# First feed-forward product in pairs of 64-row products on doubled features, with the attention numerators and the output projection moved to the second product

## Chip, cores and metric

The kernel runs on one core of a Trainium2 chip. The metric is device microseconds of one execution, as the median of several timed runs. Engines are TensorE (PE, with its weight loads as PEld), VectorE (DVE), ScalarE (ACT), GpSimd (POOL) and SyncE (SP), which issues nearly all DMAs.

## What is computed

The reference is one transformer block over 2048 tokens of 576 features, 32 heads of 18, feed-forward width 4608. A conditioning vector c gives six vectors that scale, shift and gate. Cut to what matters:

```python
sa, ca, ga, sb, cb, gb = split(silu(c) @ w_mod, 6)
h = layernorm(x) * (1 + ca) + sa
x = x + ga * attention(h)          # per head, feature map softmax(q w), softmax(-q w);
                                   # num = phi_q (phi_k^T v), den = phi_q sum(phi_k); (num / den) @ wo
h = layernorm(x) * (1 + cb) + sb
x = x + gb * (maximum(h @ w1, 0) @ w2)
```

## The kernel before

**Stages.** A first stage (to about 91 us) follows a hand-written list of jobs, ORDER: projections for K, V and Q of all 16 token tiles of 128, the key sums, and the numerators, output projection, second normalisation and h of tiles 0 and 1. The softmaxed Q of later tiles are written to DRAM (q_out, L334) and read back (q_in, L337). Then a loop over eight blocks b of two tiles (256 tokens) does the feed-forward part. Block b runs l1 (the first product, L691) and l2 (the second, L724); the attention rest of the next two tiles is hooked into them.

**The first product.** Hidden features are cut into 36 chunks of 128, taken as 18 pairs j and j+18 (hf = 0, 1). The 576 features of h are four chunks of 128 and one of 64. l1_full (L667) multiplies the four full chunks (L673, 128 rows, 256 columns). l1_rest (L676) multiplies the last 64: h's 64 features lie twice, in partitions 0 to 63 and 64 to 127, and the weights w1b hold one half of the hidden features in each, so that two products of 64 rows (L680), one for each hf, run beside each other in the two halves of the array. Three groups g of six j each use bank pairs 0 to 2 of PSUM; in each group first a part of the full products, then all six L680 pairs, then the rest of the full products with relu (L683) after each u: ScalarE writes A11 (L687) and A2 (L688), VectorE U3 (L689), and after a group U2 (L711).

**The second product** uses a Strassen scheme: seven products of 18 matmuls (L735) with sums of the halves of A and of w2: T1 to T4 are differences of weights (t_part, L461), made by VectorE in block 0, A11 and A12 are changed in place by VectorE (L743, L747, L755). Bank X accumulates four products; ScalarE takes a snapshot of it after three of them (copy, L739). fin (L713) adds, gates and writes the results with VectorE (L718, L720) and GpSimd (L721, L722).

**Attention work in the loop.** q_next (L786) makes a tile's softmax sums and ratios (VectorE L282, L341; GpSimd L344, L289) and a DMA transpose into ET. attend (L795) is ten small matmuls (num_mm, L389), a division (num_o, L396 and L397), a copy of the last 64 features by ScalarE (L800), and a DMA transpose into oT. wo_rest and wo_full (L803, L810) project: a pair of 64-row products (L807) and eight full ones (L813). add_res (L411), bn (L238, L239) and norm2 (L816) normalise; a DMA transpose of five chunks puts the result into h2, and VectorE scales and shifts it (L851) in l2. Before, hooks place attend twice in l1 of the block ahead, the projections in its groups 1 and 2, and the scaling and q_next in l2.

**What sets the order.** The program's order is the order on each engine: every engine works its instructions in the order in which the code emits them, waiting on semaphores for data and for buffers. In ORDER the jobs ht (turn2, L526: transposes by TensorE), ha and hd (h2_e, L532: scale and shift by ScalarE and VectorE) make h of tiles 0 and 1 in bank pairs 2 (tile 1) and 0 (tile 0), just ahead of the Q projection of tile 15 (bank pair 1; Q of tile 14 is in pair 3) and the loop.

## Time and profile before

| | us |
|---|---|
| three timed runs | 387.99, 387.81, 387.46 (median 387.81) |
| profiled execution: its span | 386.3 |
| first product of block 0 starts | 91.28 |
| second product, blocks 0, 1 and 2, in the chain | 112.72, 149.44, 186.15 |
| one l2 (126 matmuls) | 15.4 |
| one l1 with the attention work in it | 21.3 |

The time of a run is that of the whole execution; the span runs from the first instruction of the program to the last, and 1.5 us of the median lie around it. In the rows of the profile, "x" counts instructions, then come busy us and the mean ns of one, then idle time before them and what released them. In the chain that ended last, a row is a start, a length and the work. PEld rows are weight loads, which run beside matmuls. A matmul's row is longer than the step to the next one, because matmuls overlap in the array: 0.273 against 0.109 us for L673. So steps, not rows, add up to TensorE's time.

### The profile page before, as it was taken

The numbers are of one execution on the slowest core, as the hardware profiler recorded it, in microseconds if no ns is written. First come the engines' busy times: TensorE is split into PE (matmuls) and PEld (weight loads), VectorE is DVE, ScalarE is ACT, GpSimd is POOL, SyncE is SP. The second block draws the span as 40 slices with busy tenths as digits, with TensorE's granted clock in tenths as the row PEclk, the third lists the DMA queues.
The fourth block names the chain that finished last, engine by engine and source line by source line (L and its number), as shares of the span: only waits on it lengthen the run. The fifth ranks groups of instructions, "written<-read, shape, count | busy, mean of one in ns | idle before, by whom it ended". The sixth has DMA issues, their size and how long they took to land.

```text
span 386.3 us, 8923 instructions
## 1 busy us (share of the span) xinstructions
PE 379.6 (98%) x3705; PEld 309.7 (80%) x3705; DVE 242.6 (63%) x470; ACT 156.7 (41%) x380; POOL 125.3 (32%) x195
## 2 busy tenths in 40 slices
PE   7999999999999999999999999999999999999995
PEld 4887778888887887788888888887888788778874
DVE  2898998784898666744764584567456735542333
ACT  2689997688540233034303420451054023302510
POOL 2088889830106400620160035004500540041023
PEclk9999999999999999999999999999999999999999
DMA  7995799798510524241233024212631221200001
GB/s 301 420 417 209 261 394 360 137 259 277 84 34 19 75 53 51 47 110 34 50 76 82 20 49 110 48 19 52 122 36 20 46 63 36 36 0 32 3 0 34
DMA packets 48940, 43.18 MB, mean 112 GB/s; under 512 B 39297, under 2 KB 41986, under 8 KB 48130
## 3 DMA queue, kind: packets, MB, share of 16 engines
q1 hardware_dynamic: 48610, 42.41, 39.4%
q8 instruction: 29, 0.48, 0.5%
q10 hardware_dynamic: 288, 0.19, 0.2%
q14 instruction: 13, 0.11, 0.1%
HBM read 27.38 MB, written 5.90 MB: 86 GB/s over the span
## 4 chain that ended last, share of the span: by engine, by line
PE 87%; DMA 4%; ACT 4%; DVE 3%; issue 1%; POOL 1%; SPq 0%; POOLq 0%; DVEq 0%
PE PS L673 33%; PE PS L735 31%; PE PS L272 9%; PE PS L680 5%; PE PS L813 4%; ACT RT L277 3%; DMA x_sb<-in_xk_dram 2%; PE PS L389 2%; DMA R<-in_wkT_dram 2%; PE PS L322 1%; DVE Rk L282 1%; PE PS L406 1%; DVE st L238 1%; ACT RT L511 0%; PE PS L807 0%
## 5 line engine op out<-in xcount | busy, mean ns | idle before, releaser
L673 PE MATMUL PS<-h,R 128*128 128x256 bf16 x1152 | 132.1, 273 | 0.0
L673 PEld LDWEIGHTS <-R 128*128 128x128 bf16 x1152 | 111.4, 98 | 14.1 <-issue 0.6
L735 PEld LDWEIGHTS <-RH 128*128 128x128 f16 x846 | 82.7, 98 | 20.7
L721 POOL TENSOR_TENSOR yt<-yt,gb_row 128x288 f32<-128x288 f32 x23 | 28.0, 1219 | 202.7 <-DVE yt L720 202.7
L687 ACT ACTIVATE RH<-PS 128x256 f16<-128x256 f32 x72 | 27.5, 382 | 110.6 <-PE PS L680 92.3
L735 PE MATMUL PS<-R,RH 128*128 128x288 bf16 (+1 forms) x558 | 72.1, 286 | 0.0
L689 DVE SCALAR_TENSOR_TENSOR RH<-PS,RH 128x256 f16<-128x256 f32 x72 | 28.6, 412 | 61.0 <-ACT RH L687 61.0
L688 ACT ACTIVATE RH<-PS 128x512 f16<-128x512 f32 x72 | 42.9, 596 | 5.5 <-PE PS L673 4.6
L277 ACT ACTIVATE RT<-PS,rs 128x576 bf16<-128x576 f32 x64 | 42.8, 742 | 2.3 <-PE PS L272 1.8
L735 PE MATMUL PS<-RT,RH 128*128 128x288 f16 x288 | 37.9, 286 | 0.0
L739 ACT ACTIVATE RS<-PS 128x288 f32<-128x288 f32 x24 | 9.8, 410 | 65.2 <-PE PS L735 65.2
L272 PE MATMUL PS<-RH,R 116*128 116x288 bf16 x240 | 32.5, 286 | 0.1
L272 PE MATMUL PS<-RH,RT 116*128 116x288 bf16 x240 | 31.9, 286 | 0.3
L720 DVE TENSOR_TENSOR yt<-PS,RS 128x288 f32<-128x288 f32 x23 | 10.5, 455 | 31.0 <-PE PS L735 21.9
L238 DVE BATCH_NORM_STATS2 st<-x_sb 128x6 f32<-128x288 bf16 x64 | 25.9, 447 | 4.0 <-DMA x_sb<-in_xk_dram 3.4
L272 PEld LDWEIGHTS <-RT 116*128 116x128 bf16 x240 | 22.9, 98 | 6.0 <-issue 0.5
L272 PEld LDWEIGHTS <-R 116*128 116x128 bf16 x240 | 22.7, 98 | 6.0 <-issue 0.5
L722 POOL TENSOR_TENSOR x_sb<-yt,x_sb 128x288 bf16<-128x288 f32 x31 | 22.7, 731 | 2.9 <-DVE yt L718 1.1
L282 DVE TENSOR_REDUCE Rk<-RT 128x64 f32<-128x1152 bf16 x16 | 21.3, 1336 | 0.9 <-ACT RT L277 0.7
L282 DVE TENSOR_REDUCE Rq<-RT 128x64 f32<-128x1152 bf16 x16 | 21.5, 1343 | 0.0
L680 PE MATMUL PS<-h,R 64*128 64x256 bf16 x288 | 19.9, 271 | 0.0
L411 DVE TENSOR_TENSOR x_sb<-x_sb,PS 128x576 bf16<-128x576 bf16 x16 | 12.1, 754 | 11.3 <-PE PS L813 10.2
(119 smaller groups left out, 418.8 us busy)
## 6 DMA issues: line engine op xcount, KB each, us to landing
R<-in_w1a_dram SPq DMA_DIRECT2D x4, 1152.0 KB, 8.2
eqd<-RT SPq DMA_DIRECT2D x12, 288.0 KB, 2.1
RT<-eqd SPq DMA_DIRECT2D x12, 288.0 KB, 3.5
R<-in_w2b_dram SPq DMA_DIRECT2D x2, 1296.0 KB, 8.1
R<-in_w2a_dram SPq DMA_DIRECT2D x3, 864.0 KB
out_dram<-x_sb SPq DMA_DIRECT2D x15, 144.0 KB, 2.1
RT<-in_xT_dram SPq DMA_DIRECT2D x2, 640.0 KB, 14.0
x_sb<-in_xk_dram SPq DMA_DIRECT2D x3, 288.0 KB
```

Source lines behind the costliest of these rows:

```text
L238: dve.bn_stats(out=s[:, hf, :], in_=x_sb[:, t, hf * HD:(hf + 1) * HD])
L272: pe.matmul(pr[:, k, 0:HD], lhsT=xt(t, ck), rhs=w[0:R, ck, k * HD:(k + 1) * HD], start=(ck == 0), stop=(ck == NC - 1))
L277: act.activation(out=E.rearrange("p (b h s e) -> p b h s e", b=2, s=2, e=DH)[:, :, :, s, :], in_=pr[:, :, 0:HD].rearrange("p b (h e) -> p ...
L282: dve.tensor_reduce(out=Rr, in_=E.rearrange("p (c e) -> p c e", e=DH), axis=AXX, op=ALU.add)
L673: pe.matmul(PS[:, 2 * u + hf, n * 256:n * 256 + 256], lhsT=w1a[:, ci, jj * P:(jj + 1) * P], rhs=hb[:, ci, :], start=(n == 0 and ci == 0), ...
L680: pe.matmul(PS[:, 2 * u + hf, n * 256:n * 256 + 256], lhsT=w1b[b0:b0 + 64, j * P:(j + 1) * P], rhs=hb[b0:b0 + 64, 4, :], start=False, stop ...
L687: act.activation(out=A11[:, j, :], in_=lo[:, :, 0, :], func=ACT.Relu)
L688: act.activation(out=A2[:, j, :, :], in_=PS[:, 2 * u + 1, :].rearrange("p (n s f) -> p n s f", n=2, s=2), func=ACT.Relu)
L689: dve.scalar_tensor_tensor(out=U3[:, j, :], in0=lo[:, :, 1, :], scalar=0.0, in1=A11[:, j, :], op0=ALU.max, op1=ALU.subtract)
L721: pool.tensor_tensor(out=y, in0=y, in1=gb_row[:, c], op=ALU.mult)
L722: pool.tensor_tensor(out=x_sb[:, t, c], in0=y, in1=x_sb[:, t, c], op=ALU.add)
L735: pe.matmul(PS[:, bank, 0:HD], lhsT=am[:, j, :], rhs=bm[:, j, :], start=first and j == 0, stop=(j % 9 == 8), skip_group_check=True)
```

## The change

All of the first product is done in pairs of 64 rows. The 576 features are nine chunks of 64; each lies in h2 twice, in partitions 0 to 63 and 64 to 127, and w1 holds the first half of the hidden features in partitions 0 to 63 and the second half in 64 to 127. For each j there are nine pairs (l1_mm) in place of eight full products and one pair. l1 goes through nine groups of two j, each with a bank pair of its own, in the order 2, 1, 0, 3, ... (in block 0: 2, 1, 2, 1, 0, 3, 0, 3, 2). The first group of block 0 goes chunk by chunk over both j.

Normalised tiles are written with every 64 features twice (two VectorE operations of 576 in place of one of 576 and one of 64), so that transposes are of nine chunks: nine by TensorE for each of tiles 0 and 1, nine-chunk DMA transposes later. The modulation vectors lie in mod2 in two arrangements, of which the other half is filled by two small DMAs. The scale and shift of h2 moves from VectorE (five operations a block) to ScalarE (h_scale, nine).

From block 0 on, attend of two tiles stands in l2 (at its positions 3 and 5 of 14, a position being nine matmuls) instead of l1; the projection of both tiles stands after l2, ahead of the next l1, full products first and then the pairs, in bank pairs 3 and 0; the residual, statistics and normalisation follow in that l1's first groups and q_next in its groups 5 and 6. So tiles are prepared one block earlier than before. In block 0, tiles 2 and 3 still go through l1: attend at group 2, projection at group 6, residuals at 7, normalisation at 8 and at the start of l2. Banks X, Y and Z of l2 become 2, 4 and 3. The reserve for DMA descriptors is set to 1024 bytes a partition.

The diff, cut to its core:

```diff
...
 NK = NJ // 2
+NS = D // 64
 G7 = ((0, 7), (7, 7), (14, 7), (21, 7), (28, 4))
...
 oc0 wo3 wo4 W1:1 xr1 lb1 sq8 Q11:3 eQ10 W0:1 xr0 w2b1 eQ9 lb0 eQ11 sq11 Q12:2 lr1 Q13:1 eQ12 sq9 qi5 qi4 lr0
-eQ13 ap1 ap0 Q14:3 sq13 ht1:2 ht0:0 ha1 hd1 ha0 hd0 Q15:1 sq10 sq12 eQ15 sq15 qi6 eQ14 sq14
+eQ13 ap1 ap0 Q14:3 sq13 ht1:2 ht0:0 ha hd Q15:1 sq10 sq12 eQ15 sq15 qi6 eQ14 sq14
 """
...
     ca1 = small([P, NC], FP32, "ca1")
-    mod2 = small([P, 2, NC], FP32, "mod2")
+    mod2 = small([P, 2, 2, NC], FP32, "mod2")
     eps_t = small([P, 1], FP32, "eps_t")
...
     oT = small([P, 2, NC, P], BF16, "oT")
-    xn = small([P, 2, 640], BF16, "xn")
-    h2 = small([P, 2, NC, 2 * P], BF16, "h2")
+    xn = small([P, 2, NS * P], BF16, "xn")
+    h2 = small([P, 2, NS, 2 * P], BF16, "h2")
     gt = small([P, 2, D // 4], BF16, "gt")
...
                               op0=ALU.subtract, op1=ALU.mult)
-        cols(xn[:, t % 2, 0:D], x_sb[:, t, :])
-        cols(xn[:, t % 2, D:640], x_sb[:, t, 512:D])
+        o = xn[:, t % 2, :].rearrange("p (c d f) -> p c d f", d=2, f=64)
+        for d in range(2):
+            cols(o[:, :, d, :], x_sb[:, t, :].rearrange("p (c f) -> p c f", f=64))
     G5, FW = 504, 72
...
             eng.tensor_copy(out=wk[0:R, ck, 0:G5], in_=PS[0:R, ck, 0:G5])
-    w1a = carve(R1, 0, (4, DFF))
-    w1b = R1[:, 4 * DFF:]
+    w1 = carve(R1, 0, (NS, DFF // 2))
     w2 = [carve(R2[i], 0, (NK, D)) for i in range(2)]
...
     yl = RE[:, 0:2 * HD].bitcast(FP32)
-    X, Y, Z = 6, 4, 7
+    X, Y, Z = 2, 4, 3
     T_AT = {1: (3, 0), 2: (3, 1), 3: (3, 2), 6: (2, 0), 7: (2, 1), 8: (2, 2)}
...
     def turn2(src, pr):
-        for ci in range(NC):
+        for ci in range(NS):
             c = slice(ci // 2 * P, ci // 2 * P + P)
             pe.transpose(bf(pr[:, ci % 2, :])[:, c], src[:, ci * P:(ci + 1) * P], ident[:, 0:P])
-    def h2_e(i, pr, eng):
-        odd = int(eng is act)
-        pt = bf(pr[:, odd, :])
-        for n, ci in enumerate(range(odd, NC, 2)):
-            o, p = h2[:, 0, ci, i * P:(i + 1) * P], pt[:, n * P:(n + 1) * P]
-            if odd:
-                act.activation(out=o, in_=p, func=ACT.Identity, scale=mod2[:, 1, ci:ci + 1], bias=mod2[:, 0, ci:ci + 1])
-            else:
-                dve.tensor_scalar(out=o, in0=p, scalar1=mod2[:, 1, ci:ci + 1], scalar2=mod2[:, 0, ci:ci + 1],
-                                  op0=ALU.mult, op1=ALU.add)
+    def mod(k, c):
+        return mod2[:, c % 2, k, c // 2:c // 2 + 1]
+
+    def h2_e(odd):
+        for ci in range(odd, NS, 2):
+            for i in (1, 0):
+                p = bf(at["ht", i][:, odd, :])[:, ci // 2 * P:ci // 2 * P + P]
+                o = h2[:, 0, ci, i * P:(i + 1) * P]
+                if odd:
+                    act.activation(out=o, in_=p, func=ACT.Identity, scale=mod(1, ci), bias=mod(0, ci))
+                else:
+                    dve.tensor_scalar(out=o, in0=p, scalar1=mod(1, ci), scalar2=mod(0, ci), op0=ALU.mult, op1=ALU.add)
     def w2a_part(k):
...
     def w1_part(i):
-        if i < 4:
-            sp.dma_start(R1[:, i * DFF:(i + 1) * DFF], a["w1a"][:, i * DFF:(i + 1) * DFF])
-        else:
-            sp.dma_start(R1[:, 4 * DFF:], a["w1b"])
+        c = slice(i * DFF, min(R1.shape[1], (i + 1) * DFF))
+        sp.dma_start(R1[:, c], a["w1"][:, c])
     def mod2_e(pr):
-        act.activation(out=mod2[:, 0, :], in_=pr[:, 0, 0:NC], func=ACT.Copy)
-        act.activation(out=mod2[:, 1, :], in_=pr[:, 0, NC:2 * NC], func=ACT.Copy, bias=1.0)
+        for h in range(2):
+            r = slice(64 * h, 64 * h + 64)
+            act.activation(out=mod2[r, h, 0, :], in_=pr[r, 0, 0:NC], func=ACT.Copy)
+            act.activation(out=mod2[r, h, 1, :], in_=pr[r, 0, NC:2 * NC], func=ACT.Copy, bias=1.0)
+        for h in range(2):
+            sp.dma_start(mod2[64 - 64 * h:128 - 64 * h, h], mod2[64 * h:64 * h + 64, h])
     def kz():
...
         "ht": lambda i: turn2(xn[:, i, :], at["ht", i]),
-        "hd": lambda i: h2_e(i, at["ht", i], dve), "ha": lambda i: h2_e(i, at["ht", i], act),
+        "hd": lambda: h2_e(0), "ha": lambda: h2_e(1),
         "tp": lambda k: t_part(0, k),
...
         JOBS[f](*(() if n is None else (n,)))
-    def l1_full(js, u, cis, hb):
-
-        for hf in range(2):
-            for n, j in enumerate(js):
-                jj = j + hf * NK
-                for ci in cis:
-                    pe.matmul(PS[:, 2 * u + hf, n * 256:n * 256 + 256], lhsT=w1a[:, ci, jj * P:(jj + 1) * P],
-                              rhs=hb[:, ci, :], start=(n == 0 and ci == 0), stop=False, skip_group_check=True)
-
-    def l1_rest(js, u, hb):
+    def l1_mm(js, u, hb, chunks):
+
         for n, j in enumerate(js):
-            for hf in range(2):
-                b0 = 64 * hf
-                pe.matmul(PS[:, 2 * u + hf, n * 256:n * 256 + 256], lhsT=w1b[b0:b0 + 64, j * P:(j + 1) * P],
-                          rhs=hb[b0:b0 + 64, 4, :], start=False, stop=False, skip_group_check=True)
+            for c in chunks:
+                for hf in range(2):
+                    b0 = 64 * hf
+                    pe.matmul(PS[:, 2 * u + hf, n * 256:n * 256 + 256], lhsT=w1[b0:b0 + 64, c, j * P:(j + 1) * P],
+                              rhs=hb[b0:b0 + 64, c, :], start=(n == 0 and c == 0), stop=False, skip_group_check=True)
     def relu(js, u):
...
         dve.scalar_tensor_tensor(out=U3[:, j, :], in0=lo[:, :, 1, :], scalar=0.0, in1=A11[:, j, :], op0=ALU.max, op1=ALU.subtract)
-    def l1(b, hooks):
+    def l1(b, pairs, hooks):
         hb = h2[:, b % 2]
-        for g in range(3):
-            hooks(g, -1)
-            js = [[6 * g + 2 * u, 6 * g + 2 * u + 1] for u in range(3)]
-            cut = (4, 2, 1)
-            for u in range(3):
-                l1_full(js[u], u, range(cut[u]), hb)
-                if u == 0:
-                    hooks(g, "first")
-            for u in range(3):
-                l1_rest(js[u], u, hb)
-            hooks(g, "rest")
-            for u in range(3):
-                l1_full(js[u], u, range(cut[u], 4), hb)
-                relu(js[u], u)
-                if b == 0 and g == 1:
-                    t_part(1, u)
-                hooks(g, u)
-            j = slice(6 * g, 6 * g + 6)
-            dve.tensor_tensor(out=U2[:, j, :], in0=U3[:, j, :], in1=A22[:, j, :], op=ALU.add)
+        for u in range(9):
+            hooks(u)
+            js = [2 * u, 2 * u + 1]
+            if b == 0 and u == 0:
+                for c in range(NS):
+                    l1_mm(js, pairs[u], hb, [c])
+            else:
+                l1_mm(js, pairs[u], hb, range(NS))
+            relu(js, pairs[u])
+            if u % 3 == 2:
+                j = slice(2 * u - 4, 2 * u + 2)
+                dve.tensor_tensor(out=U2[:, j, :], in0=U3[:, j, :], in1=A22[:, j, :], op=ALU.add)
     def fin(t, k, bank, s):
...
             held.append(q + NL)
-    def attend(t):
-        pr = pair(3)
+    def attend(t, pr):
         num_mm(t, pr)
         num_o(t, pr)
-        if t > 1:
-            act.activation(out=o_sb[:, t % 2, D:640], in_=o_sb[:, t % 2, 512:D], func=ACT.Copy)
+        act.activation(out=o_sb[:, t % 2, D:640], in_=o_sb[:, t % 2, 512:D], func=ACT.Copy)
         turn_dma(oT[:, t % 2], o_sb[:, t % 2, :])
-
-    def wo_rest(t, pr):
-
-        for k in range(2):
-            b0 = 64 * k
-            pe.matmul(pr[:, k, 0:HD], lhsT=oT[b0:b0 + 64, t % 2, 4, :], rhs=wo_sb[b0:b0 + 64, 4, k * HD:(k + 1) * HD],
-                      start=True, stop=False, skip_group_check=True)
     def wo_full(t, pr):
...
                 pe.matmul(pr[:, k, 0:HD], lhsT=oT[:, t % 2, ci, :], rhs=wo_sb[:, ci, k * HD:(k + 1) * HD],
-                          start=False, stop=(ci == 3), skip_group_check=True)
-
-    def norm2(b, t):
+                          start=(ci == 0), stop=False, skip_group_check=True)
+
+    def wo_rest(t, pr):
+
+        for k in range(2):
+            b0 = 64 * k
+            pe.matmul(pr[:, k, 0:HD], lhsT=oT[b0:b0 + 64, t % 2, 4, :], rhs=wo_sb[b0:b0 + 64, 4, k * HD:(k + 1) * HD],
+                      start=False, stop=True, skip_group_check=True)
+
+    def project(t, prs):
+        for i in range(2):
+            wo_full(t + i, prs[i])
+        for i in range(2):
+            wo_rest(t + i, prs[i])
+
+    def residual(t, pr):
+        add_res(t, pr)
+        bn(1, t)
+
+    def norm2(t):
         ln2_rs(t)
...
         i = t % 2
-        turn_dma(h2[:, (b + 1) % 2, :, i * P:(i + 1) * P], xn[:, i, :])
+        turn_dma(h2[:, t // 2 % 2, :, i * P:(i + 1) * P], xn[:, i, :])
+
+    def h_scale(b, k):
+        for c in range(3 * k, 3 * k + 3):
+            o = h2[:, b % 2, c, :]
+            act.activation(out=o, in_=o, func=ACT.Identity, scale=mod(1, c), bias=mod(0, c))
+
+    WO = (pair(3), pair(0))
+
+    def b0_l1(u):
+        if u == 1:
+            q_next(4)
+        if u == 2:
+            attend(2, pair(3))
+            attend(3, pair(0))
+            q_next(5)
+        if u in (4, 5, 6):
+            t_part(1, u - 4)
+        if u == 6:
+            project(2, (pair(2), pair(1)))
+        if u == 7:
+            residual(2, pair(2))
+            residual(3, pair(1))
+        if u == 8:
+            norm2(2)
+
+    def in_l1(b):
+        t = 2 * b + 2
+
+        def hook(u):
+            if t < NT:
+                if u == 0:
+                    for i in range(2):
+                        add_res(t + i, WO[i])
+                if u in (1, 2):
+                    bn(1, t + u - 1)
+                if u in (3, 4):
+                    norm2(t + u - 3)
+            if u in (5, 6):
+                q_next(min(t + u - 3, NT))
+        return hook
+
+    def in_l2(b):
+        t = 2 * b + 2
+
+        def hook(pos):
+            if b == 0 and pos == 0:
+                norm2(3)
+            lag = 6 if b == 0 else 0
+            if t < NT and pos - lag in (1, 3, 5):
+                h_scale(b + 1, (pos - lag) // 2)
+            if t + 2 < NT and pos in (3, 5):
+                attend(t + 2 + pos // 5, WO[pos // 5])
+        return hook
     for b in range(NB):
-        t0 = 2 * b + 2
-        more = b + 1 < NB
-
-        def in_l1(g, u):
-            if not more:
-                return
-            if (g, u) in (((0, 0), (1, "first")) if b == 1 else ((0, 0), (0, 2))):
-                attend(t0 + int(u in (2, "first")))
-            if b == 0 and (g, u) == (1, "first"):
-                q_next(t0 + 2)
-            if g and u == "rest":
-                wo_rest(t0 + g - 1, pair(3))
-            if g and u == 0:
-                t = t0 + g - 1
-                wo_full(t, pair(3))
-                add_res(t, pair(3))
-                bn(1, t)
-            if (g, u) == (1, 2):
-                norm2(b, t0)
-
-        def in_l2(pos):
-            if not more:
-                return
-            if pos == 1:
-                norm2(b, t0 + 1)
-            if pos == (8 if b else 12):
-                hb = h2[:, (b + 1) % 2]
-                for ci in range(NC):
-                    dve.tensor_scalar(out=hb[:, ci, :], in0=hb[:, ci, :], scalar1=mod2[:, 1, ci:ci + 1],
-                                      scalar2=mod2[:, 0, ci:ci + 1], op0=ALU.mult, op1=ALU.add)
-            if pos in ((4, 10) if b else (12,)):
-                q_next(t0 + 2 + int(pos > 4))
-
-        l1(b, in_l1)
-        l2(b, in_l2)
+        l1(b, (2, 1, 2, 1, 0, 3, 0, 3, 2) if b == 0 else (2, 1, 0, 3, 2, 1, 0, 3, 2), in_l1(b) if b else b0_l1)
+        l2(b, in_l2(b))
+        if 0 < b + 1 and b + 2 < NB:
+            project(2 * b + 4, WO)
 def _rows():
...
     o["wo"] = flat(wo.reshape(NC, P, D).transpose(1, 0, 2))
-    w1 = g["B_w1"]
-    o["w1a"] = flat(w1[:512].reshape(4, P, DFF).transpose(1, 0, 2))
-    o["w1b"] = np.concatenate([w1[512:, :DFF // 2], w1[512:, DFF // 2:]], axis=0)
+    w1 = g["B_w1"].reshape(D // 64, 64, 2, DFF // 2)
+    o["w1"] = flat(w1.transpose(2, 1, 0, 3).reshape(P, D // 64, DFF // 2))
     w2 = g["B_w2"].reshape(NJ, P, D).transpose(1, 0, 2)
...
     from concourse.bass_utils import run_bass_kernel_spmd as _run
-    nc = _bacc.Bacc("TRN2", target_bir_lowering=False, num_devices=1)
+    nc = _bacc.Bacc("TRN2", target_bir_lowering=False, num_devices=1, dynamic_dma_scratch_size=1024)
     lay = _layout(inputs)
```

## The prediction

> **What bounds the kernel now.** I read the page's busy shares first, then the chain that ended last, then that chain over one steady block, then the order of time at the seams.

> ```profile
> PE 379.6 (98%) x3705; PEld 309.7 (80%) x3705; DVE 242.6 (63%) x470; ACT 156.7 (41%) x380; POOL 125.3 (32%) x195
> PEclk9999999999999999999999999999999999999999
> PE 87%; DMA 4%; ACT 4%; DVE 3%; issue 1%; POOL 1%; SPq 0%; POOLq 0%; DVEq 0%
> L680 PE MATMUL PS<-h,R 64*128 64x256 bf16 x288 | 19.9, 271 | 0.0
> ```

> TensorE is busy throughout at full clock. From 91.28 us on (first product, block 0) the chain of waits is PE alone until the tail at 378, so only PE time and waits put into PE count there. One steady block in the chain:

> ```profile
> 201.59 3.06 PE PS L673 x28
> 204.64 0.76 PE PS L680 x12
> 205.40 0.48 PE PS L389 x10
> ...
> 213.47 5.24 PE PS L673 x48
> 218.71 0.76 PE PS L680 x12
> 219.47 0.12 PE PS L807 x2
> 219.59 1.09 PE PS L813 x8
> 220.68 2.18 PE PS L673 x20
> 222.87 15.43 PE PS L735 x126
> ```

> A full product steps at 5.24/48 = 0.1092 us, one of the second product at 15.43/126 = 0.1225. Six pairs of L680 take 0.76, not 6 x 0.109 = 0.655. The order of time shows why:

> ```profile
> 210.68 0.82 PE L673 MATMUL PS<-h,R 128*128 128x256 bf16 x6
> 211.43 0.55 PEld L680 LDWEIGHTS <-R 64*128 64x128 bf16 x12 [0.21 <-issue]
> 211.43 0.83 PE L680 MATMUL PS<-h,R 64*128 64x256 bf16 x12
> 212.10 0.28 PE L807 MATMUL PS<-wo_sb,oT 64*128 64x288 bf16 x2
> 212.32 1.16 PE L813 MATMUL PS<-wo_sb,oT 128*128 128x288 bf16 x8
> 213.31 0.27 PE L673 MATMUL PS<-h,R 128*128 128x256 bf16 x1
> ```

> Six full products need 211.43 - 210.68 = 0.75, which is 0.10 over their 0.655; the six pairs 0.67 (0.01 over); the 64-row pair of L807 0.22 where a pair of 288 columns takes 0.12 (0.10 over); the next eight 0.99 (0.01 over). So a pair inside a run costs 0.109, what one full product costs, and going from full array to halves and back costs 0.21: the first weight load of the new kind waits 0.21 for its start ("issue").

> **The change, part by part** (times are starts in the trace of before, moved on).

> *Multiplications.* Before, a block has 144 full products and 18 pairs; after, 162 pairs. At 0.109 each the sum is the same: 0.

> *Switches.* Before: 24 runs of halves, each with an entry and an exit (three a block). The built order of after has 10: three in block 0 (numerators and projection still stand inside its first product) and one in each of seven blocks. 14 x 0.213 = **-2.98**.

> *Nine transposes a tile instead of five, block 0.* They start at 89.14; first step 0.06, 17 more at 0.0555 (five took 0.28 in the chain), so the last starts at 90.09 and Q15's projection at 90.15 instead of 90.00: **+0.15**.

> *Doubled features of block 0.* h2_e has 8 ScalarE operations instead of 4, 10 on VectorE instead of 6:

> ```profile
> 89.63 1.60 DVE L540 TENSOR_SCALAR h<-PS,mod 128x128 bf16<-128x128 bf16 x6 [0.27 <-PE PS L530]
> 89.83 1.50 ACT L538 ACTIVATE h<-PS,mod 128x128 bf16<-128x128 bf16 x4
> ```

> ScalarE steps at 0.34 (four in 1.50, the last 0.47 long). In after its second operation waits for the second tile's last transpose, 90.09 + 0.27 = 90.36. The first group of pairs writes bank pair 2, where tile 1's transposes still lie; its second matmul therefore waits for the seventh ScalarE operation: 90.36 + 5 x 0.342 + 0.47 + 0.05 for the semaphore = 92.59. PE is done with Q15 at 91.37, or 91.47 with the switch. **+1.12**, less the 0.07 that PE waited here before. The VectorE side is done by 92.3. Doing this product chunk by chunk hides only the eighth operation. The two exponentials of Q15 and Q14 move to 92.8-95.2 on ScalarE; bank pairs 1 and 3 are wanted at 94.6 and 96.6: hidden.

> *First second product, block 0.* VectorE carries more here. Rows used: L689 412, L411 754, L238 447, L420 423, L465 1051, L743 1358, L396 353, L397 758 ns; an operation whose result the next doesn't need frees VectorE 0.085 sooner (190.70 L720, 0.46 long, next at 191.07). Let e be the end of the seventh group's pairs; the residual of tiles 2 and 3 is queued behind that group's L689. That one starts at e+0.63 (semaphore 0.21, L687 0.38, 0.03) and frees at 0.92; two residuals with statistics 2 x 1.77: 4.46; L689 0.29 and tile 2 normalised 0.68: 5.43; the last L689 and its U2 sum 0.89: 6.32; tile 3 0.68: 7.00; a T3 part 0.97; A11 1.27; two T3 parts 1.94: 11.18; numerators of tile 4 1.07 and the first result 0.37: 12.62; tile 5 0.39 + 0.76: 13.77. Behind that stand on ScalarE tile 5's pad copy (0.03 + 0.16) and the second snapshot of bank X (0.41), and PE's fifth product writes X: e+14.42. PE would be there at e + 36 x 0.109 + 0.11 + 6.615 + 2 x 0.383 + 1.10 = 12.52. **+1.90**. T4 and A12, later, have slack.

> *The same place in blocks 1 to 5.* A11 starts at 2.41 after the product's start (188.39 - 185.99), first result at 4.71 + 0.38 = 5.09, A12 at 5.47, tile's reciprocal 6.73, product 7.12 to 7.88, pad copy and snapshot to 8.48, PE at 8.53 against its own 8.48: 5 x 0.05 = **+0.25**. From below 0; from above A12 may lose its place to PoolE (rival 2).

> *At nothing.* Numerators and projection keep their matmuls, 0.038 and 0.1225 each, in either place. The scaling of h, 35 x 504 ns on VectorE, becomes 63 operations on ScalarE at about 0.41 (L511: five in 2.1), 3.7 a block, between snapshots in a product of 15.4 where ScalarE is busy 2.2. First-product groups: VectorE's residuals, statistics, normalising and two softmax sums (2 x 1.65) with nine L689 end at about 19.2 us of a block whose A11 sum is wanted at 20.2; if that cover is gone PE waits at the fourth product. A bank pair comes round after 7.9 us. SP's queue: h transposes of nine chunks cost at most the 3.7 to landing of today's nine-chunk ones, issued at 9 and 10 us and wanted at 18.8; the second q_turn waits behind a q_in that needs the first's landing: about 22 us, wanted at 23.7; outputs stand behind oT as before. The two mod2 transfers and two more ScalarE copies come near 27 us, ahead of an 0.8 us ScalarE gap. The smaller descriptor scratch: all transfers come from SP and ACT, none from PoolE: 0, unmeasured.

> Sum: -2.98 + 0.15 + 1.12 - 0.07 + 1.90 + 0.25 = **+0.37** on the profiled execution's span of 386.3. The timed median of before is 387.81, 1.5 above that span, in which nothing here is changed: 388.2.

> **Rivals.**
> 1. *The waits are shorter than walked.* Then the switches win. For: every term of the two big waits is a chain of rows with no slack counted in my favour. Against: each releaser is fixed by the order on its engine. With all waits gone 387.81 - 2.98 + 0.08 = 384.9; with half of them 386.5.
> 2. *Slower: the second snapshot of X is late in each of blocks 1 to 5.* My chain meets PE with no margin, so it decides from 0.05 us on and passes every delay on. The price: PoolE's product of the first result (L721) starts beside A12's subtraction. In before VectorE kept the way and L721 took 1.78 in place of 0.73; where PoolE was first (L289 at 194.49) a VectorE operation of 0.34 took 1.3. If PoolE goes first, 0.73 x 5 = 3.6: 391.8; with half the blocks 390.0.
> 3. *Long runs of pairs are slower than six.* No run in before is longer. 1152 more pairs at 1 to 5 ns: 1.2 to 5.8, so 389.4 to 394.
> 4. *PE's issue.* A pair is two couples of weight load and matmul; if issuing a couple takes c, a long run of pairs is bound once 2c passes 0.109. A full product leaves 0.109 for one couple, so before hides this, and twelve couples may lie ready in the queue. The nearest long row:

> ```profile
> 24.09 0.77 PE L249 MATMUL PS<-siluc,RE 116*128 116x1 bf16 x25
> 24.72 0.76 PE L249 MATMUL PS<-siluc,R 116*128 116x1 bf16 x25
> 25.35 0.32 PE L257 MATMUL PS<-RS,R 126*116 126x126 bf16 x3
> ```

> 50 couples in 25.35 - 24.09 = 1.26: c is 0.025. Against that stands only the transposes' 0.0555; were that issue and not streaming, 1152 x 0.002 = 2.3, 390.5 or more. [...]
> 5. *The change doesn't do what it says*: halves still pay the switch somewhere. The built order shows 10 runs; if waits inside runs cost as much as switches, 391.

> **How the numbers follow.** Forecast 0.47, rival 1 0.18, rival 2 0.22, rival 3 0.08, rival 4 0.03, rival 5 0.02. The forecast's own range is 387.2 to 389.2 (0.5 us on each of the two walks). For eight in ten I leave out the ends of rivals 1 and 2 (0.05, 0.04), the upper half of 3 and all of 4: 385.6 to 391.0. 0.2%, about what a measurement can tell from no change, is 0.78: faster below 387.03 holds rival 1 and 0.03 of the forecast, 0.21; within holds 0.34 of the forecast, 0.03 of rival 2 and 0.02 of rival 3, 0.39; slower the rest, 0.40.

> **What would show it.** A steady block (start to start of the second product) of 36.34 instead of 36.71; 162 pairs at 0.109; PEld waits for issue at 20 places (ten in, ten out) instead of 48; a first pair at 92.6 whose releaser is ScalarE's h operation; a PE gap near 1.9 in the second product of block 0, released by the snapshot copy. Wrong if pairs step above 0.110, if PE waits in blocks 1 to 5 for more than 0.3, or if block 0's gap is missing.

## The result, and the profile after

The changed kernel took 390.3 us (median of seven runs, 388.88 to 390.83), the kernel before 387.98 beside it (seven runs, 387.46 to 388.5): a ratio of 1.0048, 95% interval 1.0031 to 1.0065 (estimated from all runs; the quotient of the two medians is 1.006). That is slower by about half a per cent. The forecast was 388.2, with 385.6 to 391.0 as its range. The seven runs fall into two groups by the granted clock: three took 388.88 to 389.10 at a mean clock of 0.998 to 1.000, four took 390.30 to 390.83 at 0.994 to 0.995. The profiled execution is of the second group (span 388.8).

From the profile page of the changed kernel: the busy shares, the clock line, the engines of the chain that ended last, and two groups of matmuls.

```profile
PE 379.3 (98%) x4863; PEld 313.8 (81%) x4865; DVE 240.6 (62%) x439; ACT 186.2 (48%) x449; POOL 122.0 (31%) x195
PEclk9999999999999899999999999999999999999999
PE 85%; DVE 5%; ACT 4%; DMA 2%; issue 1%; POOL 1%; SPq 0%; POOLq 0%; DVEq 0%; ACTq 0%
L678 PE MATMUL PS<-h,R 64*128 64x256 bf16 x2592 | 143.2, 269 | 1.0 <-DVE h L544 1.0
L726 PE MATMUL PS<-R,RH 128*128 128x288 bf16 (+1 forms) x558 | 74.8, 290 | 2.3 <-ACT RS L730 2.3
```

TensorE is as full as before in the total. Three things are new: an 8 in the clock line, a wait of 1.0 ahead of the first pairs, and one of 2.3 in the second product; the matmuls of both products had 0.0 before. The last is one single wait, at 122.25 us, in block 0. The chain over a steady block of the changed kernel (start, length, work) has none:

```profile
190.75 3.41 PE PS L726 x27
194.16 0.38 PE PS L390 x10
...
197.12 9.96 PE PS L726 x81
207.08 1.96 PE PS L795 x16
209.04 0.35 PE PS L802 x4
209.39 17.68 PE PS L678 x324
```

The 162 pairs (324 matmuls) take 17.68, 0.1091 each. From second product to second product a block takes 36.33 us on the mean (190.684 to 227.008 by the first matmuls in this one), against 36.71 before. So the steady blocks gained 0.38 each, as forecast, and the time came back elsewhere. By stations, after against before: the first pair starts 1.42 later (92.70), the second product of block 0 1.33 later, the one of block 1 5.08 later (154.35 against 149.28), and from there the kernel catches up: 2.72 later at block 7, 2.52 at the end.

The loss between the second and the third station is all in block 0's second product: 2.50 and 1.7 us, as the next rows show, less the 0.4 that two switches fewer save. The idle waits of TensorE between 90 and 380 us in the changed kernel (total, times, longest):

```profile
PE PS L726 <- ACT RS L730: 2.3, 1, 2.3
PE PS L678 <- DVE h L544: 1.0, 1, 1.0
```

L730 is the snapshot of bank X on ScalarE. In that queue stands what held it (order of time, ScalarE; the brackets are the idle time before an instruction and its releaser):

```profile
122.85 0.26 ACT L789 ACTIVATE o_sb<-o_sb 128x64 bf16<-128x64 bf16 x1 [6.13 <-DVE o_sb L398]
124.27 0.26 ACT L789 ACTIVATE o_sb<-o_sb 128x64 bf16<-128x64 bf16 x1 [1.17 <-DVE o_sb L398]
124.43 0.39 ACT L730 ACTIVATE RS<-PS 128x288 f32<-128x288 f32 x1
```

The last matmul of the sum in bank X ended at 121.43, and TensorE would write the bank again at about 122.4. But the snapshot of the sum stands behind two pad copies, which wait for the scaled numerators of tiles 4 and 5 (L398), which stand on VectorE behind residuals, normalisations, T3 (L466) and A11 (L734):

```profile
117.59 0.24 DVE R L466
...
118.47 1.35 DVE RH L734
119.82 1.94 DVE R L466 x2
121.76 0.28 DVE rden L397
...
123.48 0.77 DVE o_sb L398
...
124.43 0.40 ACT RS L730
```

That is the chain of the prediction. Steps say what it costs: the matmul after it starts 2.62 after its predecessor, 2.50 more than the usual 0.1225. Then comes what no row of before had (windows of the changed kernel; us, TensorE's busy time, and so on, with the granted clock before the last two columns):

```profile
122.25:124.87 2.62, 0.29 (x3) 0.10 (x1) 2.59 (x5) 0.85 (x4) 1.46 (x2) 1.00 0.24 55
125.00:128.42 3.42, 3.42 (x16) 2.19 (x15) 3.42 (x4) 1.29 (x3) 0.00 (x0) 0.50 0.22 48
```

For 3.41 us after the pause the clock is 0.50. L726 steps at 0.240 there, so 1.7 us of it are lost. Those 1.7 are the distance between the medians of the two groups of runs (388.9 and 390.6).

### The profile page after: what moved, and what is told of

The parts are those of the page before. It is cut to its first block, busy times and chain, and to the rows that moved or that the text cites. A ratio compares the mean times of both kernels' runs of the same rounds, so it can differ in the third digit from the quotient of the medians.

```text
span 388.8 us, 11323 instructions
## 1 busy us (share of the span) xinstructions
PE 379.3 (98%) x4863; PEld 313.8 (81%) x4865; DVE 240.6 (62%) x439; ACT 186.2 (48%) x449; POOL 122.0 (31%) x195
## 4 chain that ended last, share of the span: by engine, by line
PE 85%; DVE 5%; ACT 4%; DMA 2%; issue 1%; POOL 1%; SPq 0%; POOLq 0%; DVEq 0%; ACTq 0%
PE PS L678 35%; PE PS L726 29%; PE PS L273 11%; PE PS L795 4%; ACT RT L278 2%; DMA R<-in_wsh_dram 2%; PE PS L390 1%; PE PS L323 1%; DVE st L239 1%; PE PS L250 1%; PE PS L802 1%; PE PS L407 1%; DVE R L466 1%; DVE h L544 1%; PE PS L258 0%
## 5 line engine op out<-in xcount | busy, mean ns | idle before, releaser
L678 PE MATMUL PS<-h,R 64*128 64x256 bf16 x2592 | 143.2, 269 | 1.0 <-DVE h L544 1.0
L678 PEld LDWEIGHTS <-R 64*128 64x128 bf16 x2592 | 126.6, 94 | 16.4 <-issue 1.4
L726 PEld LDWEIGHTS <-RH 128*128 128x128 f16 x846 | 82.5, 99 | 25.5 <-issue 4.2
L726 PE MATMUL PS<-R,RH 128*128 128x288 bf16 (+1 forms) x558 | 74.8, 290 | 2.3 <-ACT RS L730 2.3
L712 POOL TENSOR_TENSOR yt<-yt,gb_row 128x288 f32<-128x288 f32 x23 | 24.1, 1048 | 138.1 <-DVE yt L711 138.1
L687 DVE SCALAR_TENSOR_TENSOR RH<-PS,RH 128x256 f16<-128x256 f32 x72 | 29.4, 415 | 44.7 <-ACT RH L685 44.7
L278 ACT ACTIVATE RT<-PS,rs 128x576 bf16<-128x576 f32 x64 | 42.9, 745 | 2.2 <-PE PS L273 1.8
L726 PE MATMUL PS<-RT,RH 128*128 128x288 f16 x288 | 37.9, 286 | 0.0
L345 POOL TENSOR_TENSOR ratq<-Rq,rq 128x32 f32<-128x32 f32 x16 | 4.0, 253 | 93.5 <-DVE rq L342 93.5
L824 ACT ACTIVATE h<-h,mod 128x256 bf16<-128x256 bf16 x63 | 32.8, 590 | 0.0
L730 ACT ACTIVATE RS<-PS 128x288 f32<-128x288 f32 x24 | 9.8, 406 | 28.3 <-PE PS L726 28.3
```

Of the source, the lines that this page charges most:

```text
L278: act.activation(out=E.rearrange("p (b h s e) -> p b h s e", b=2, s=2, e=DH)[:, :, :, s, :], in_=pr[:, :, 0:HD].rearrange("p b (h e) -> p ...
L678: pe.matmul(PS[:, 2 * u + hf, n * 256:n * 256 + 256], lhsT=w1[b0:b0 + 64, c, j * P:(j + 1) * P], rhs=hb[b0:b0 + 64, c, :], start=(n == 0 a ...
L687: dve.scalar_tensor_tensor(out=U3[:, j, :], in0=lo[:, :, 1, :], scalar=0.0, in1=A11[:, j, :], op0=ALU.max, op1=ALU.subtract)
L712: pool.tensor_tensor(out=y, in0=y, in1=gb_row[:, c], op=ALU.mult)
L726: pe.matmul(PS[:, bank, 0:HD], lhsT=am[:, j, :], rhs=bm[:, j, :], start=first and j == 0, stop=(j % 9 == 8), skip_group_check=True)
L824: act.activation(out=o, in_=o, func=ACT.Identity, scale=mod(1, c), bias=mod(0, c))
```

## The experiments

Theory: the switches gained what was forecast, and the snapshot in block 0's second product, held by the order on VectorE and ScalarE, gives it back, with a half clock behind it when the pause is long. Rivals: TensorE pauses for a reason of its own there; the half clock comes from the work and not from the pause; the steady gain comes from the pairs and not from fewer switches. Each run has the kernel before beside it on its chip (388.27, with e10, e12 and e13 388.12, with e14 388.14), and ratios are to that.

### e1_late: tile 5's attention two positions later

```diff
-            if t + 2 < NT and pos in (3, 5):
+            if t + 2 < NT and pos in ((3, 7) if b == 0 else (3, 5)):
```

> Block 0's attend of tile 5 moves from position 5 to position 7 of the second product, so that ScalarE takes the second snapshot of bank X ahead of tile 5's pad copy; nothing else changes. Queue theory: PE's gap of 2.6 us ahead of the fifth product goes, about 0.3 us comes back where A12 is late, and with no long gap the clock stays full in every run: 388.9 (the runs of the changed kernel at full clock) - 2.5 + 0.3 = 386.7, all runs within 0.4. Rival, that VectorE's backlog is the bound and not the queue: PE waits as long for T4 or A12 further on, and the time stays at 388.6 to 390.3.

Measured: 388.25 (11 runs), 1.0002 [0.9993, 1.0010]. The expected 386.7 did not come. The waits of TensorE in it:

```profile
PE PS L726 <- ACT RS L730: 1.3, 2, 0.9
```

The wait split in two: the snapshot now stands only behind tile 4's pad copy, which was late too (123.24), and the next snapshot behind tile 5's (127.13). By steps 1.66 of the 2.50 remain. The releaser is right and the remedy was too small: the whole chain on VectorE is late, not tile 5's part alone. No execution was at half clock (0.998 or more in all eleven).

### e2_spin10 and e6_spin4: the pause filled with matmuls

These multiply zeros into bank 5, ten (e6: four) matmuls of 512 columns, ahead of the waiting product; nothing of the kernel's own work is moved.

```diff
+            if b == 0 and pos == 7:
+                spin(10, 5)
```

> Ten matmuls of zeros (512 columns, a free bank) stand ahead of the fifth product of block 0, where PE waits: 10 x 0.216 = 2.2 us of the 2.6 us gap are filled, no result changes. Idle theory: the half clock after the gap comes from PE's idleness; all runs are then at clock 1.000 and at 388.8 to 389.3, none near 390.6. Rival, that the clock falls for another reason (the 64-row pairs, or a rhythm of its own): runs at 0.994 and 390.5 appear as before, about every second one.

> Four matmuls of zeros instead of ten at the same place: 0.9 us of the gap filled, 1.7 us of idleness left. If a gap of 1.7 us is too short to lower the clock, all runs are at 388.8 to 389.3 and clock 1.000. If the idle share of a window decides gradually, some runs still show 0.994 and 390.5.

Measured: 389.05 (ten runs), 1.0023 [1.0014, 1.0032], and 389.2 (ten runs), 1.0024 [1.0015, 1.0033]; clocks of 0.998 or more in all twenty. The order of time on TensorE in e2_spin10 (nine of the ten are in the trace):

```profile
122.64 2.11 PE L234 MATMUL PS<-zero 128*128 128x512 bf16 x9
124.93 2.37 PE L726 MATMUL PS<-R,RH 128*128 128x288 f16 x18 [0.18 <-ACT RS L730]
```

The product still starts at 124.9: the snapshot sets it, not TensorE. But the half clock is gone, and with it 1.7 us in the executions that had it. Four spins leave an idle wait of 1.5, and that brought no half clock either. So the half clock follows the pause, and it costs time beside what the pause itself costs.

### e3_tile1: tile 1's scaled features ahead of tile 0's

```diff
-        for ci in range(odd, NS, 2):
-            for i in (1, 0):
+        for i in (1, 0):
+            for ci in range(odd, NS, 2):
```

> The doubled features of block 0 are made for tile 1 first and then for tile 0, instead of in turns by chunk, so that the bank pair of the first group comes free after four ScalarE operations instead of seven. Bank theory: the first pair starts near 91.6 instead of 92.7, the chunks of tile 0 arrive as fast as PE takes them: 1.0 to 1.1 us less in every run, 387.8 at full clock and 389.4 with the half-clock window. Rival, that the supply of chunks is the bound (17 operations in two queues): the wait moves behind the first chunks and the gain is under 0.3.

Measured: 390.0 (8 runs), 1.0033 [1.0017, 1.0048]; three runs at 388.14 to 388.67, five at 389.97 to 390.4 with clocks of 0.994 to 0.996. The first pair starts at 91.66 instead of 92.70, but its second group then waits 0.41 for ScalarE (the exponentials of Q15, L278, which no longer fit in front), so about 0.6 of the 1.04 is left (0.55 between the medians of the full-clock runs, 388.35 and 388.90, which stood beside different runs of the kernel before). The start of block 0 was set by these eighteen scalings, eight on ScalarE and ten on VectorE, as forecast; what stands behind them on ScalarE is late next. The pause at 122 is unchanged here, 2.3, and the one traced execution runs at half clock after it.

### e7_t3 and e8_t3_tile1: T3 out of the chain

T3's three parts (L466) are made in block 0's first product, group 6, instead of next to A11 in its second product, ahead of the numerators. e8 has e3's order of h as well.

```diff
-    T_AT = {1: (3, 0), 2: (3, 1), 3: (3, 2), 6: (2, 0), 7: (2, 1), 8: (2, 2)}
+    T_AT = {6: (2, 0), 7: (2, 1), 8: (2, 2)}
...
+            for k in range(3):
+                t_part(3, k)
             project(2, (pair(2), pair(1)))
```

> The three T3 parts (2.9 us of VectorE work) move from the second product of block 0 to the seventh group of its first product, where VectorE waits 2.2 us; nothing else changes. Queue theory: the divisions of tiles 4 and 5 end 2.7 us sooner, the snapshots behind the pad copies are no longer late, PE's gap of 2.6 us goes wholly and with it the half-clock window: 2.5 us under the changed kernel at full clock (about 389.1 beside this before, 388.3), so 386.6, all at clock 0.998 or more, ratio near 0.9957. Rival, that another VectorE result (A11, T4, A12) takes the gap's place: 387.5 or more, with a PE gap of 1 us or more in that product.

> The T3 parts early and the doubled features for tile 1 first, together. If the two waits are independent, the second adds the 0.6 us that it gained alone (first pair 1.04 us sooner, 0.41 given back where the second group waits for Q15's exponentials): 386.0, ratio near 0.994. If the earlier start only lengthens a later wait: 386.6.

Measured: 387.18 (8 runs), 0.9974 [0.9963, 0.9984], and 387.08 (5 runs), 0.9968 [0.9955, 0.9980]. Taking these 2.91 us off the chain removes the wait for the snapshot, and the changed kernel becomes faster than the one before. But e7_t3 stays 0.6 above the expected 386.6. Against the full-clock runs of the changed kernel it is 2.0 of the 2.50 (0.9 above its kernel before, now 1.1 below). The chain of e7_t3 shows the rest:

```profile
108.58 2.91 DVE R L466 x3
111.49 0.33 DVE RH L687
111.83 0.67 DVE x_sb L412
112.50 0.04 issue
112.54 2.14 PE PS L678 x36
```

The three parts in one piece hold a relu (L687) and a residual (L412), and TensorE waits 0.36 (a step of 0.467 instead of 0.105) at 112.5 for the bank pair that the residual reads; a step of 0.224 at 116.7, in the second product, is 0.10 more. e8_t3_tile1 is only 0.1 below e7_t3 by the medians and misses both of its forecasts (386.0 and 386.6): its first pair starts at 91.72, but steps of 0.531 at 94.1 and 0.744 at 111.9 follow, so most of the earlier start went into later waits.

### e9_switch: one more switch in each projection

e7_t3, with the projection of two tiles as full, pair, full, pair instead of full, full, pair, pair.

```diff
-        for i in range(2):
```

> The T3 parts early, and in each of the seven projections the pairs of the first tile go ahead of the full products of the second: full, pairs, full, pairs. Same matmuls, one more passage to halves and back each. Switch theory: 7 x 0.213 = 1.49 us more than the kernel with T3 early, 388.1. Rival, that a switch costs only where weights were not ready anyway: under 0.5 us more.

Measured: 388.42 (11 runs), 1.0010 [1.0000, 1.0019], 1.24 over e7_t3. The chain of a steady block in it, where e7_t3 has 1.96 for sixteen and 0.35 for four:

```profile
203.72 0.98 PE PS L795 x8
204.70 0.23 PE PS L802 x2
204.93 1.09 PE PS L795 x8
206.01 0.23 PE PS L802 x2
```

The same twenty matmuls take 2.53 instead of 2.31, and a block 36.54 instead of 36.33: a way into halves and back costs 0.21, as read off before. That is 1.28 for the six projections behind a second product. The seventh, in block 0's first product, costs nothing (21.57 from first to second product in both), because TensorE waits for the residual there in e7_t3 and no such wait is left in e9_switch.

### e11_alone: pairs, but the numerators and projection inside the first product

e7_t3, with attention, projection and residuals of every block at groups 2, 6 and 7 of the first product, as in block 0. So each block again has three runs of halves.

> The pairs alone: T3 early as before, but numerators, projection and residuals of each next pair of tiles stand inside the first product of every block, as the changed kernel has it in block 0 alone; the same operations. Runs of halves: 22 instead of 10. If the gain of this change is the switches and not the pairs themselves: 12 x 0.213 = 2.6 us above the kernel with T3 early, 389.2, level with or above before. If the pairs gain by themselves: 387 or less.

Measured: 389.37 (5 runs), 1.0032 [1.0020, 1.0045], 2.19 over e7_t3. A steady block of it, in the chain:

```profile
207.49 0.86 PE PS L390 x20
208.35 7.97 PE PS L678 x144
216.31 2.07 PE PS L795 x16
```

From second product to second product it takes 36.71 (151.132 to 187.845), what the kernel before takes. So all pairs instead of mostly full products is worth nothing by itself; the 0.38 a block comes from moving the numerators and the projection, that is, from two round trips less. Two of them are 0.43; the changed order gives 0.04 back at the late snapshot of each of blocks 1 to 5, which e11_alone does not have. That is also why e11_alone lies 2.2 and not the expected 2.6 above e7_t3.

### e10_contig: where the normalised tile is written

The changed kernel with each copy of a normalised tile written in one piece. It leaves out the order of the features that the weights expect; the work is the same.

```diff
-        o = xn[:, t % 2, :].rearrange("p (c d f) -> p c d f", d=2, f=64)
         for d in range(2):
-            cols(o[:, :, d, :], x_sb[:, t, :].rearrange("p (c f) -> p c f", f=64))
+            cols(xn[:, t % 2, d * D:(d + 1) * D], x_sb[:, t, :])
```

> The changed kernel, but the two copies of a normalised tile are written as two contiguous blocks of 576 columns instead of alternating runs of 64. The features of h then stand in other places than the weights expect, so the output is that of wrongly arranged features; the amount of work is the same. Theory: the normalise operation costs 0.56 us instead of 0.42 because of where it writes. Then it takes about 423 ns here, a step of 0.34, the four of them ahead of block 0's first snapshot give 4 x 0.14 = 0.56, the first pair is at about 92.6 and TensorE's wait in block 0's second product shrinks from 2.50 to about 1.95 us. Rival: the cost is one of the size or of the neighbours; the operation stays at 0.56 and the wait at 2.5. A wait of 1.95 would also say whether a half clock still follows it: with 1.7 us of idle time left in two pieces (the run that held tile 5 back) there was none.

Measured, in one execution: 388.03, 1.000 of the median beside it. VectorE's normalisations between 85 and 130 us (count; busy us, mean ns of one; idle before), in the changed kernel and in e10_contig:

```profile
L421 DVE TENSOR_SCALAR xn<-x_sb,mv,rs 128x576 bf16<-128x576 bf16 x8 | 4.1, 559 | 0.3 <-ACT rs L416 0.3
```

```profile
L421 DVE TENSOR_SCALAR xn<-x_sb,mv,rs 128x576 bf16<-128x576 bf16 x8 | 3.0, 419 | 0.6 <-ACT rs L416 0.6
```

The layout costs 0.14 an operation, and the step at the pause is 2.07 instead of 2.62, what four of them make (0.56). The first pair starts at 92.35, below the expected 92.6: the wait of tile 0's transposes (0.18) is gone, and this start scatters from 92.62 to 93.09 anyway in the traces of kernels that are the same up to there. In this one execution the clock stayed at 1.00 after a pause of 1.94.

### e12_spread and e13_spread_tile1: each third of T3 right after T1's

```diff
         if u in (4, 5, 6):
             t_part(1, u - 4)
+            t_part(3, u - 4)
```

> As the kernel with the third difference (T3) made in block 0's first product, but each third of it right after the same third of T1 (groups 4, 5 and 6) instead of all three in group 6. In the kernel with all three in group 6 VectorE ran from 107.5 to 111.4 without a break, a relu came late by that, and TensorE waited 0.34 us at 112.5 (a step of 467 ns). Theory: that wait goes and nothing takes its place: 0.3 us under it, 386.9, a ratio of about 0.9965 to the kernel before. Rival: the backlog only moves to the numerators and residuals of tiles 2 and 3 behind it, and the wait comes earlier or as a wait in the second product: 387.2, 0.9973.

> The same, with tile 1's scaled features all made ahead of tile 0's (as in the run that did this with the changed kernel). With T3 all in group 6, that gave a first pair at 91.72 instead of 93.04 but waits of 0.41 us after the first group and 0.6 us at 111.9, and 0.1 us in all. Theory: the second of these waits was VectorE's backlog and goes: 386.6, a ratio of 0.9957. Rival: the waits are set by the exponentials and not by the backlog: 387.0, 0.997.

Measured: 387.03 (10 runs), 0.9975 [0.9966, 0.9984], and 386.7 (5 runs), 0.9963 [0.9950, 0.9977]. The first is no better than e7_t3: the step at 112.3 is still 0.417 instead of 0.467, since the last thirds of T1 and T3 together still stand in front of that residual. So the theory of these two runs held for 0.05 of the wait. e13_spread_tile1 keeps both waits of e8 (steps of 0.532 at 94.1 and 0.738 at 111.9): its time is near the expected 386.6, but the wait that was to go did not, so it came out by luck. Its interval overlaps with those of e7, e8 and e12.

### e14_oneop: both copies of a tile in one normalisation

e13_spread_tile1, with one operation of 1152 columns for a tile instead of two of 576; the copy is the outermost dimension of its output.

```diff
-        o = xn[:, t % 2, :].rearrange("p (c d f) -> p c d f", d=2, f=64)
-        for d in range(2):
-            cols(o[:, :, d, :], x_sb[:, t, :].rearrange("p (c f) -> p c f", f=64))
+        cols(xn[:, t % 2, :].rearrange("p (c d f) -> p d c f", d=2, f=64),
+             x_sb[:, t, :].rearrange("p (c f) -> p c f", f=64).unsqueeze(1).to_broadcast([P, 2, NS, 64]))
```

> The kernel with T3 spread and tile 1 first, with the two normalising operations of a tile (576 columns each, written in nine runs of 64) made one of 1152 columns whose outermost dimension is the copy (two of nine runs of 64). The contiguous writing took 0.42 us and the one in nine runs 0.56. The runs of 64 are the same in all of these; what differs is the outermost dimension of the output, 576 in one run, nine, or now two. Theory: the odd nine is what costs, at half the rate: then the 0.14 between them is the contiguous one's time for 576 columns and 0.28 is fixed, and the one operation takes 0.28 + 2 x 0.14 = 0.56. [...] Rival: the short runs themselves cost, whatever stands outside: 0.28 + 2 x 0.28 = 0.84. For the whole kernel the first gives up to 0.4 us of VectorE a tile; where it shows is tile 0's transposes (0.18 late ahead of the first pair) and the waits at 94 and 112: 386.4, a ratio of 0.9955. The second gives 0.1 a tile and no change, 386.7, 0.9963.

Measured: 386.49 (5 runs), 0.9964 [0.9950, 0.9977] to 388.14. The normalisations between 85 and 130 us in e14_oneop, the same columns as in the fences of e10_contig:

```profile
L421 DVE TENSOR_SCALAR xn<-x_sb,mv,rs 128x1152 bf16<-128x1152 bf16 x4 | 2.3, 564 | 0.8 <-ACT rs L416 0.8
```

Twice the columns take 564 ns, what one operation of 576 took in the changed kernel (559). That is the 0.56 of the theory and not the 0.84 of the rival: in these rows the runs of 64 cost nothing, and the order with the nine outermost costs 0.14 an operation (559 against 419). Whether it is the odd number that costs, as the theory has it, they do not show. In the kernel's time little of it is left, 0.2 us under e13_spread_tile1 by the medians and no difference between the ratios (0.9964 and 0.9963). The first pair starts at 91.41 instead of 91.74, and the wait behind it, for the exponentials, grows (a step of 0.667 for 0.532). It is the fastest kernel here by its median, 1.65 us under the one before.

## Why the prediction was right, and where not

- **Switches, -2.98: right.** In the trace after, ten steps out of halves are 0.201 to 0.202 where a pair takes 0.109, and eight of those into halves are 0.218 to 0.219. The steady block is 36.33 (36.34 forecast); from block 1's second product to block 7's it is 214.97 (215.02 forecast). e9_switch and e11_alone put it on the switches.
- **Pairs at 0.109 in a long run: right.** Rivals 3, 4 and 5 fall: the 162 pairs of a steady block take 17.68 us in the trace after, 0.109 each, so neither the length of the run nor TensorE's issue bounds a pair here, and no switch is paid inside it.
- **First pair at 92.59: 92.70.** Mis-sized by 0.11, the normalisation again: tile 0's transposes waited 0.18 for it (a step of 0.234 at 89.82). The releaser shown is VectorE's h operation; ScalarE's seventh ended 0.05 later and freed the second matmul, so the two sides came closer together than I had walked. By the walk the seventh ends at 92.54; it ended at 92.69.
- **Block 0's snapshot, +1.90: mechanism right, 2.50 measured.** The mis-sized term is the normalisation of tiles 2 and 3. I took L420's 423 ns of before for each of the two operations (0.34 a step). With an output of alternating runs of 64 they take 562 (0.48), and four of them make 0.56 of the 0.60. e10_contig and e14_oneop show it.
- **What failed: no term for the clock.** The prediction has the granted clock at full speed on both sides of the wait. In the traced execution the pause of 2.50 was followed by 3.41 us at 0.50, which cost 1.7; by their mean clock, four of the seven had that. With full clock the kernel is at 388.9, 0.7 over the forecast, which is the two mis-sized terms (0.11 + 0.60); with the half clock it is at 390.6. The median fell among the latter. It lies outside the forecast's own range of 387.2 to 389.2, and inside 385.6 to 391.0 only because that was held wide for slower rivals, of which none came true. That the time is in the range is luck.
- **Blocks 1 to 5, +0.25: right.** The step at that place is 0.161 to 0.164 instead of 0.123, 0.04 each. Rival 2 (PoolE ahead of A12) did not happen in any of the five. Rival 1 fell too: the big waits were longer than walked, not shorter.
- **At nothing.** h_scale is 590 ns (a step of 0.49), not 0.41, and stayed hidden; ScalarE has 48% now. No first-product group waits in blocks 1 to 7. Not forecast: the tail from block 7's second product on is 19.53 instead of 19.73. I did not follow that up.

Together: forecast +0.37 on the span, measured +2.52; 0.11 + 0.60 + 1.70 - 0.05 - 0.20 make 2.16 of the 2.15 between them.

## What to carry to other kernels

Count the changes between full-array and half-array matmuls, not the halves: a long run of half-array pairs costs what full products cost (0.109 us each), and each way in and back costs 0.21 us here. When work moves into a stage that feeds TensorE through another engine's queue, walk that queue for the first block too, where the neighbours differ; one subtraction moved earlier (e7_t3) turned this change from 1.0048 to 0.9974. Check what an operation costs with the layout that it will write (e14_oneop halves it by another order of the same dimensions), and count a TensorE pause of some 2.5 us as one that can cost more than its length (2.50 and 1.70 behind it here).

## What the runs showed of the chip that was not expected

A TensorE pause can cost 1.7 times its length (2.50 and 1.70 behind it). With an idle wait of 2.3 us (the changed kernel and e3_tile1) 9 of 15 executions had a mean clock of 0.994 to 0.996, and the two of these that were traced have the half clock right behind the pause. With 1.8 (e10_contig, one execution) and 1.5 (e6_spin4, ten) there was none. In the changed kernel the half clock lasted 3.413 us; in e3_tile1 the windows of 122 to 126 and 126 to 130 us have a mean clock of 0.82 and 0.76, which makes about 3.4 us at half clock as well.

One execution of e9_switch in eleven had 0.995 too (390.24 us); the one traced has no idle wait after the first pairs, so that case stays open.

A VectorE normalisation of 576 bf16 columns takes 559 ns into nine runs of 64 and 419 into one run, and one of 1152 into two times nine runs takes 564. Why the order with the nine outermost is the slower one, no run shows.
